# Attention transfers gathered on one queue, in the order of need

## The chip, the cores and the metric

The kernel runs on one core of a Trainium2 chip. The time is device microseconds of one execution. Five engines work side by side, each with its own instruction stream: TensorE (matrix products), VectorE, ScalarE, GpSimd and SyncE. In this kernel SyncE does nothing but start transfers between HBM and the on-chip memory (SBUF); ScalarE and GpSimd start some as well, between their computations. An engine starts its instructions in order, so an instruction that waits holds up all that stand behind it.

## The reference, cut to what matters

First a block-sparse attention over 4 sequences of 768 tokens with 8 heads of 64; a query block of 32 tokens sees its own block and both neighbours, the first and the last block of the sequence, and three sampled blocks:

```python
scores = scale * np.matmul(q, k.transpose(0, 1, 3, 2))
mask = np.abs(blk_i - blk_j) <= 1
mask = mask | (blk_i == 0) | (blk_j == 0) | (blk_i == n_blocks - 1) | (blk_j == n_blocks - 1)
for qb in range(n_blocks):
    for kb in sampled_blocks[qb]:
        mask[qb * 32:(qb + 1) * 32, kb * 32:(kb + 1) * 32] = True
scores = np.where(mask, scores, -1e9)
attn = softmax(scores)
x = np.matmul(attn, v)                      # then (B, H, S, D) -> (B*S, H*D): 3072 rows of 512
```

Then each of the 3072 rows goes to one of 8 experts, chosen by the cosine between the row and the experts' embeddings:

```python
expert_idx = np.argmax(xn @ en.T / tau, axis=1)
gate_w = softmax(...)[np.arange(N), expert_idx]
for e in range(E):
    mask = expert_idx == e
    h = np.maximum(x[mask] @ w1[e], 0.0)    # 512 x 1024
    out[mask] = gate_w[mask, None] * (h @ w2[e])
```

All is float32.

## The kernel before, in words

The attention walks over 24 chunks of 128 queries, six to a sequence. A chunk's rows are shifted by one block, so the first chunk of a sequence holds the last block and the first three. `attention_fast` has a loop over s from 0 to 24, and its order of instructions is written out by hand: no scheduler moves anything. One iteration s scores chunk s (`score_near`, `score_far`, with the exponentials on ScalarE at L534/L540 and L559), prepares the keys of the sampled blocks for chunk s+1 (`gather_k`, on GpSimd and VectorE, L495), weighs V for chunk s-1 (`weigh_near`, `weigh_far`, all TensorE instructions at L589), turns K of the next sequence one pair of heads at a time (`turn_k`, L464/L466), turns Q of chunk s+1 (`turn_q`, L478), and normalizes chunk s-1. In a sequence's first chunk the first and the last block attend to everything (`score_ends`, L576).

Data comes in these transfers. Q: 256 KB a chunk (`load_q`, L392), in two pieces for the first chunk of a sequence, issued by ScalarE two chunks ahead into two buffers (tile `qraw`). K: two transfers of 192 KB for a pair of heads (`load_k`, L401, tile `kraw`, two buffers), by SyncE for sequence 0 and by ScalarE afterwards. V twice: once whole for a sequence (`load_v`, ten transfers, tile `vst`; L1237 for sequence 0, L1319 by ScalarE afterwards, three at the end of each iteration), with the two end blocks in a second place too (`vg0`, which the profile lists as `vg`); and once more block by block for the sampled blocks (`gather_v`, L444, SyncE): 12 transfers of 64 KB for a chunk (6 for a sequence's first) into one of three `vg` buffers, at addresses that SyncE holds in registers. The registers are loaded from the tile `offset` (L379) when a chunk's place in the sequence comes up for the first time; the addresses of the first and third slot share one register (`PACK`) and are taken apart by a shift and a mask. `near_v` (L454) copies the neighbour blocks from `vst` into `vg` on GpSimd.

Once a sequence is through, its routing runs in small steps put into later iterations by a list (`after_sequence`); its last steps write the rows with their gate to HBM (`x_dram`, L789): seven transfers of up to 258 KB, by ScalarE during attention and by SyncE after it. After sequence 1 the first 5 tiles of 128 rows for the experts are laid out; the weights of the first come in iterations 20 to 22 in eight pieces (L1078, SyncE). Then follow the expert tiles: 64 products at L1125, 16 at L1140 for each, with 4 MB of weights a tile from SyncE, and rows in and out by indirect transfers from GpSimd (L1049, L1055, L1149). The experts' embedding and tau are loaded by SyncE (`load_experts`, L208/L210) after the gathers of chunk 0 and are normalized in `build_experts` in iterations 0 and 1.

Waits are set by the framework: a reader waits for the writer, and a transfer into a buffer for the buffer's last reader.

Of the kernel before, what the change touches and what calls it, by code (L numbers as in the profile page):

```python
# [26 lines left out]
PACK = 1024  # L27
# [305 lines left out]
def build_choice(k):  # L333
# [6 lines left out]
    k.offset = k.const.tile([P, NRAND + 1, NB], I32, name="offset")  # L340
    nc.vector.tensor_scalar(out=k.offset[:, 0:NRAND, 2:], in0=at, scalar1=float(BLK), scalar2=None, op0=ALU.mult)
    nc.vector.tensor_scalar(out=at, in0=at, scalar1=float(BLK), scalar2=None, op0=ALU.mult)
    nc.vector.scalar_tensor_tensor(out=k.offset[:, NRAND, 2:], in0=at[:, 2], scalar=float(PACK), in1=at[:, 0],
                                   op0=ALU.mult, op1=ALU.add)
# [28 lines left out]
def shifts(k, engine, s, c):  # L373

    blocks = blocks_of(c)
    key = engine, s, c
    if key not in k.shift:
        most = (S - BLK) * (PACK + 1 if s == NRAND else 1)
        _, values = k.nc.values_load_multi_w_load_instructions(  # L379
            k.offset[0:1, s, NG * c + blocks[0]:NG * c + blocks[-1] + 1], engines=(engine,), min_val=0, max_val=most,  # L380
            skip_runtime_bounds_check_because="the block numbers are clamped to the blocks there are")
        k.shift[key] = list(values)
    return k.shift[key]


def load_q(k, n):

    b, c = divmod(n, NC)
    k.raw["q", n] = t = k.ld.tile([P, H, D], F32, name="qraw", tag="qraw", bufs=2)
    src = k.q[b].rearrange("h s d -> s h d")  # L390
    for rows, lo in pieces(c):
        k.nc.scalar.dma_start(out=t[rows], in_=src[lo:lo + rows.stop - rows.start])  # L392


def load_k(k, g, pool=None):
# [3 lines left out]
    for h in range(2):  # L399
        engine = k.nc.scalar if b else k.nc.sync  # L400
        engine.dma_start(out=t[:, :, h], in_=k.k[b, 2 * j + h].rearrange("(c p) d -> p c d", p=P))  # L401


def load_v(k, b):

    v, vg0 = k.vst[b % 2], k.vg0[b % 2]
# [23 lines left out]
def gather_v(k, n):  # L430
# [1119 lines left out]
```

## Time and profile before

| | |
|---|---|
| median of three runs | 715.79 us (711.06 to 717.91) |
| the profiled execution, its time | 719.66 us |
| the profiled execution, its span | 717.9 us |
| TensorE busy | 636.9 us (89%) |
| VectorE, ScalarE, GpSimd busy | 222.5, 121.4, 233.3 us |
| first score of chunks 0, 6, 12, 18 | 20.0, 107.1, 185.2, 266.8 us |
| first expert product, last one's end | 343.3, 711.1 us |
| transfers on SyncE's queue (q1) | 135.52 MB, 57.1% of 16 DMA engines' span |
| on ScalarE's queue (q10) | 20.88 MB, 13.5% |

The span goes from the first instruction to the last. A line of the profile names an engine, a line of the kernel, what is written and read, and times; an engine's name with a q (SPq is SyncE's queue, ACTq ScalarE's) is its issuing part, whose time isn't counted as busy. PE is TensorE, PEld its weight loads, DVE VectorE, ACT ScalarE, POOL GpSimd. PEclk and the column after the engines' busy times are the clock granted to TensorE, 1.00 being full.

### The profile page before, as it was taken

How to read it: one execution, taken by the hardware profiler on the slowest of the kernel's cores; microseconds unless marked ns; L12 is line 12 of the kernel's file. 1: busy time of each engine (PE TensorE's matmuls, PEld its weight loads, DVE VectorE, ACT ScalarE, POOL GpSimd, SP SyncE). 2: the span in 40 equal slices, each digit the busy share in tenths (PEclk: the TensorE clock that was granted, in tenths of full speed). 3: DMA queues.
4: the chain of work that ended last, by engine and by line, in shares of the span. 5: the costliest groups of instructions: out<-in, count | busy, mean ns of one | idle time of the engine just before them, and what ended most of it. 6: DMA issues, size and time to landing. Idle time of an engine off the chain costs nothing.

```text
span 717.9 us, 21825 instructions
## 1 busy us (share of the span) xinstructions
PE 636.9 (89%) x9016; PEld 500.4 (70%) x9016; DVE 222.5 (31%) x663; ACT 121.4 (17%) x278; POOL 233.3 (33%) x444
## 2 busy tenths in 40 slices
PE   7487789787896879985899999999999999999996
PEld 4476788776885868874766777677467773677673
DVE  6442223352253436640256111211211121112110
ACT  2312214223322415321100000000000000000000
POOL 1552124241241424450020234224322432243232
PEclk8876669979798879996889999999999999999999
DMA  9846544688436854459799999999989999899911
GB/s 169 150 105 128 104 101 91 128 142 195 115 77 139 140 137 114 115 133 267 258 399 370 396 406 367 346 345 321 342 317 396 408 393 387 315 404 397 355 34 41
DMA packets 192191, 171.33 MB, mean 239 GB/s; under 512 B 152584, under 2 KB 152712, under 8 KB 189266
## 3 DMA queue, kind: packets, MB, share of 16 engines
q1 hardware_dynamic: 119938, 135.52, 57.1%
q10 hardware_dynamic: 66928, 20.88, 13.5%
q0 software_dynamic: 5216, 13.43, 5.2%
q8 instruction: 73, 1.20, 0.7%
q14 instruction: 36, 0.29, 0.1%
HBM read 157.17 MB, written 12.90 MB: 237 GB/s over the span
## 4 chain that ended last, share of the span: by engine, by line
PE 73%; DMA 13%; DVE 4%; issue 4%; ACT 2%; SPq 2%; ACTq 1%; POOL 1%; POOLq 0%; DVEq 0%
PE hp L1125 23%; PE yp L1140 22%; PE av L589 11%; DMA vg<-in_v_dram 4%; PE yp L696 4%; DMA kraw<-in_k_dram 4%; DMA qraw<-in_q_dram 3%; PE xg_ps L478 3%; PE hp L1168 2%; PE yp L1188 2%; DVE x L672 2%; DMA x_dram<-x 1%; PE bps L576 1%; PE kps L464 1%; PE dps L554 1%
## 5 line engine op out<-in xcount | busy, mean ns | idle before, releaser
L1125 PEld LDWEIGHTS hp<-xgt,w 128*128 128x128 f32 x1472 | 167.8, 192 | 10.2 <-issue 10.2
L1125 PE MATMUL hp<-xgt,w 128*128 128x128 f32 x1472 | 168.9, 276 | 0.0
L1140 PE MATMUL yp<-w,h 128*128 128x512 f32 x368 | 163.5, 598 | 0.0
L1140 PEld LDWEIGHTS yp<-w,h 128*128 128x128 f32 x368 | 69.0, 193 | 78.1 <-issue 77.8
L1049 POOL DMA_INDIRECT xg<-x_dram,quarter x88 | 88.5, 1006 | 32.3 <-issue 27.4
L495 POOL COPY kg<-kt 128x128 f32 x176 | 45.0, 300 | 85.5 <-issue 59.9
L1149 POOL DMA_INDIRECT out_dram<-y,slot_l x20 | 20.2, 1011 | 156.8 <-DVE y L1148 156.8
L454 POOL COPY vg<-vst 32x520 f32<-32x520 f32 x80 | 49.4, 618 | 59.0 <-PE av L589 29.5
L589 PE MATMUL av<-vg,pd 128*32 128x65 f32 x1408 | 39.4, 266 | 28.3 <-DMA vg<-in_v_dram 19.9
L1128 ACT ACTIVATE h<-hp 128x512 f32<-128x512 f32 x23 | 13.7, 597 | 291.5 <-PE hp L1125 291.5
L482 DVE COPY qt<-xg_ps 64x512 f32<-64x512 f32 x48 | 33.1, 689 | 96.0 <-PE xg_ps L478 95.2
L589 PEld LDWEIGHTS av<-vg,pd 128*32 128x32 f32 x1408 | 32.6, 137 | 35.0 <-issue 13.0
L1132 DVE TENSOR_SCALAR h<-hp 128x512 f32<-128x512 f32 x23 | 15.9, 691 | 127.9 <-PE hp L1125 127.9
L589 PE MATMUL av<-vst,pac 64*64 64x65 f32 x1056 | 51.7, 243 | 1.0 <-issue 0.7
L554 PE MATMUL dps<-qt,kg 128*64 128x64 f32 x1408 | 49.5, 231 | 0.6 <-issue 0.3
L554 PEld LDWEIGHTS dps<-qt,kg 128*64 128x64 f32 x1408 | 46.1, 145 | 2.6 <-issue 0.4
L1148 DVE TENSOR_SCALAR y<-yp,gate 128x512 f32<-128x512 f32 x20 | 15.0, 751 | 102.1 <-PE yp L1140 90.1
L589 PEld LDWEIGHTS av<-vst,pac 64*64 64x64 f32 x1056 | 43.9, 153 | 3.8 <-issue 1.4
L464 PE MATMUL kps<-ident,kraw 128*128 128x128 f32 x96 | 17.8, 335 | 22.2 <-ACT pac L534 21.1
L530 PE MATMUL ac<-qt,ke 64*64 64x128 f32 (+1 forms) x384 | 33.8, 311 | 1.6 <-ACT pd L559 0.9
L559 ACT ACTIVATE pd<-dps,bias 128x256 f32<-128x256 f32 x88 | 34.6, 476 | 1.5 <-PE dps L554 1.4
L696 PEld LDWEIGHTS yp<-en,xt 128*128 128x128 f32 x192 | 32.8, 257 | 2.1 <-ACT sq L677 1.2
(228 smaller groups left out, 659.3 us busy)
## 6 DMA issues: line engine op xcount, KB each, us to landing
w<-in_moe_w_dram SPq DMA_DIRECT2D x52, 2048.0 KB, 15.7
vg<-in_v_dram SPq DMA_DIRECT2D x266, 64.0 KB, 3.2
qraw<-in_q_dram ACTq DMA_DIRECT2D x20, 256.0 KB, 3.3
kraw<-in_k_dram ACTq DMA_DIRECT2D x24, 192.0 KB, 3.8
w<-in_moe_w_dram SPq DMA_DIRECT2D x8, 512.0 KB, 4.8
x_dram<-x ACTq DMA_DIRECT2D x15, 258.0 KB, 4.4
vst<-in_v_dram ACTq DMA_DIRECT2D x15, 256.0 KB, 4.7
kraw<-in_k_dram SPq DMA_DIRECT2D x8, 192.0 KB, 5.6
```

The source lines that it names most:

```text
L454: k.nc.gpsimd.tensor_copy(out=k.vg[n][NRAND * BLK:P, g], in_=k.vst[b % 2][rows, m])
L464: nc.tensor.transpose(ps[:, c // 3, c % 3 * P:(c % 3 + 1) * P], raw[:, c].rearrange("p h d -> p (h d)"), k.ident)
L482: k.nc.vector.tensor_copy(out=t[rows, :, h], in_=ps[rows])
L495: copy(out=t[:, :, g, s * BLK:(s + 1) * BLK], in_=kt[:, :, bass.ds(shift, BLK)])
L530: nc.tensor.matmul(ps[D * r:D * (r + 1), h, lo:lo + cols.stop - cols.start], lhsT=keys, rhs=qt[rows, j, h, cols], start=True, stop=True)
L554: nc.tensor.matmul(out[D * r:D * (r + 1), NG * j + g], lhsT=kg[:, j, g, D * r:D * (r + 1)], rhs=qt[:, j, :, cols], start=True, stop=True)
L559: nc.scalar.activation(e[:, :, g].rearrange("p j h t -> p j (h t)"), out.rearrange("p (j g) h t -> p j g (h t)", g=NG)[:, :, g], ACT.Exp, ...
L589: k.nc.tensor.matmul(av[lanes, h // NPAIR, h % NPAIR * P:h % NPAIR * P + D + 1], lhsT=lhsT, rhs=rhs, start=first[0], stop=last, skip_group ...
L696: k.nc.tensor.matmul(ps[:, 0:E], lhsT=xt[:, j], rhs=k.en[:, j, :], start=(j == 0), stop=(j == ND - 1))
L1049: k.nc.gpsimd.indirect_dma_start(out=x[:, g], out_offset=None, in_=quarters, in_offset=bass.IndirectOffsetOnAxis(ap=k.quarter[:, g, t:t + ...
L1125: nc.tensor.matmul(hp[:, f, :], lhsT=w1[:, d, (f0 + f) * P:(f0 + f + 1) * P], rhs=xt[:, d, :], start=(d == 0), stop=(d == ND - 1))
L1140: nc.tensor.matmul(yp, lhsT=h[:, f, :], rhs=w2[:, f, :], start=(f == 0), stop=(f == NF - 1))
```

## The change

Every transfer of the attention but the first two chunks' Q is issued by SyncE, at the head of an iteration and in the order in which the data is needed: K, Q, the sampled blocks of V, V of the next sequence; the row writes stay at their places in the list. Q is loaded three chunks ahead into three buffers instead of two. V of a sequence comes in seven transfers instead of ten: the last and the first block lie together in `vst`, and the second copy of the two end blocks is made on chip by GpSimd (`keep_ends`). For that the end blocks change places, and the end keys `ke` are copied by two ScalarE instructions instead of one. The rows of a sequence go to HBM in four transfers instead of seven (two of them over two and three chunks, 516 and 774 KB), in three steps of the list instead of six. The packed register is gone; the third slot's four addresses are loaded anew for each chunk. The experts' embedding is loaded before V of sequence 0.

```diff
-    k.offset = k.const.tile([P, NRAND + 1, NB], I32, name="offset")
+    k.offset = k.const.tile([P, NRAND, NB], I32, name="offset")
...
-    nc.vector.tensor_scalar(out=at, in0=at, scalar1=float(BLK), scalar2=None, op0=ALU.mult)
-    nc.vector.scalar_tensor_tensor(out=k.offset[:, NRAND, 2:], in0=at[:, 2], scalar=float(PACK), in1=at[:, 0],
-                                   op0=ALU.mult, op1=ALU.add)
...
+        if engine == mybir.EngineType.SP and s == NRAND - 1:
+            return list(values)
         k.shift[key] = list(values)
...
-    k.raw["q", n] = t = k.ld.tile([P, H, D], F32, name="qraw", tag="qraw", bufs=2)
+    k.raw["q", n] = t = k.ld.tile([P, H, D], F32, name="qraw", tag="qraw", bufs=3)
...
-        k.nc.scalar.dma_start(out=t[rows], in_=src[lo:lo + rows.stop - rows.start])
+        (k.nc.scalar if n < 2 else k.nc.sync).dma_start(out=t[rows], in_=src[lo:lo + rows.stop - rows.start])
...
-        engine = k.nc.scalar if b else k.nc.sync
-        engine.dma_start(out=t[:, :, h], in_=k.k[b, 2 * j + h].rearrange("(c p) d -> p c d", p=P))
+        k.nc.sync.dma_start(out=t[:, :, h], in_=k.k[b, 2 * j + h].rearrange("(c p) d -> p c d", p=P))
...
-    for i, at in enumerate((0, S - BLK)):
-        for lo, to in ((0, v[:, 0]), (D, vg0)):
-            parts.append((to[lo + i * BLK:lo + (i + 1) * BLK, :, 0:D], src[at:at + BLK]))
-    parts.append((v[D:P, 0, :, 0:D], src[BLK:BLK + D]))
+    parts.append((v[0:BLK, 0, :, 0:D], src[S - BLK:S]))
+    parts.append((v[BLK:P, 0, :, 0:D], src[0:P - BLK]))
...
+def keep_ends(k, b):
+
+    k.nc.gpsimd.tensor_copy(out=k.vg0[b % 2][D:P], in_=k.vst[b % 2][0:D, 0])
...
-        for g, shift in zip(blocks_of(c), shifts(k, mybir.EngineType.SP, s if s == 1 else NRAND, c)):
-            if s == 0:
-                shift = shift & (PACK - 1)
-            elif s == 2:
-                shift = shift >> (PACK.bit_length() - 1)
-            if s != 1:
-                shift.max_val = S - BLK
+        for g, shift in zip(blocks_of(c), shifts(k, mybir.EngineType.SP, s, c)):
...
-        nc.scalar.copy(out=k.ke[b % 2][:, pairs].rearrange("p j (n t) -> p j n t", n=2),
-                       in_=k.kt[b % 2][:, pairs].rearrange("p j (n t) -> p j n t", t=BLK)[:, :, 0:NB:NB - 1])
+        for i, block in enumerate((NB - 1, 0)):
+            nc.scalar.copy(out=k.ke[b % 2][:, pairs, i * BLK:(i + 1) * BLK],
+                           in_=k.kt[b % 2][:, pairs, block * BLK:(block + 1) * BLK])
...
-    queue = nc.scalar if k.attending else nc.sync
-    for c in range(NC):
-        for rows, lo in pieces(c, not k.exact):
-            queue.dma_start(out=k.x_dram[b * S + lo:b * S + lo + rows.stop - rows.start, :],
-                              in_=x[rows, c].rearrange("p e w -> p (e w)"))
+    for rows, lo in pieces(0, not k.exact):
+        nc.sync.dma_start(out=k.x_dram[b * S + lo:b * S + lo + rows.stop - rows.start, :],
+                          in_=x[rows, 0].rearrange("p e w -> p (e w)"))
+    yield
+    first = b * S + P - BLK * (not k.exact)
+    for some in (range(1, 3), range(3, NC)):
+        lo = first + P * (some.start - 1)
+        nc.sync.dma_start(out=k.x_dram[lo:lo + P * len(some), :].rearrange("(c p) w -> p c w", p=P),
+                          in_=x[:, some.start:some.stop].rearrange("p c e w -> p c (e w)"))
         yield
...
-    plan += [(s + 3 + (i // 2 + 1) // 2, (i // 2 + 1) % 2, routing) for i in range(NC)]
+    plan += [(s + 3 + (i + 1) // 2, (i + 1) % 2, routing) for i in range(3)]
...
         load_k(n, g, n.setup if g < 2 else None)
+    load_experts(n)
     for to, src in load_v(n, 0):
         nc.sync.dma_start(out=to, in_=src)
...
     near_v(n, 0)
-    load_experts(n)
+    keep_ends(n, 0)
...
+        if s == 0:
+            load_q(n, 2)
+            for g in range(NPAIR, NPAIR + 2):
+                load_k(n, g)
+        if b + 1 < B and c >= 2 and NPAIR * (b + 1) + c < B * NPAIR:
+            load_k(n, NPAIR * (b + 1) + c)
+        if s + 3 < NCH:
+            load_q(n, s + 3)
         if s + 1 < NCH:
             gather_v(n, s + 1)
+        if b + 1 < B and c:
+            for to, src in load_v(n, b + 1)[2 * c - 2:2 * c]:
+                nc.sync.dma_start(out=to, in_=src)
+        if b + 1 < B and c == 2:
+            keep_ends(n, b + 1)
         if s < NCH:
             score_near(n, s)
...
-        if s == 0:
-            for g in range(NPAIR, NPAIR + 2):
-                load_k(n, g)
-        if s + 2 < NCH:
-            load_q(n, s + 2)
-        if b + 1 < B:
-            g = NPAIR * (b + 1) + c + 1
-            if 1 <= c <= NPAIR and g < B * NPAIR:
-                load_k(n, g)
-            for to, src in load_v(n, b + 1)[3 * c:3 * c + 3]:
-                nc.scalar.dma_start(out=to, in_=src)
```

More of the change, by code (lines that the diff above doesn't have):

```diff
@@ L26 @@
 NC = S // P
-PACK = 1024
 NPAIR = H // 2
@@ L377, in shifts @@
     if key not in k.shift:
-        most = (S - BLK) * (PACK + 1 if s == NRAND else 1)
         _, values = k.nc.values_load_multi_w_load_instructions(
-            k.offset[0:1, s, NG * c + blocks[0]:NG * c + blocks[-1] + 1], engines=(engine,), min_val=0, max_val=most,
+            k.offset[0:1, s, NG * c + blocks[0]:NG * c + blocks[-1] + 1], engines=(engine,), min_val=0, max_val=S - BLK,
             skip_runtime_bounds_check_because="the block numbers are clamped to the blocks there are")
+        if engine == mybir.EngineType.SP and s == NRAND - 1:
+            return list(values)
         k.shift[key] = list(values)
@@ L399, in load_k @@
     for h in range(2):
-        engine = k.nc.scalar if b else k.nc.sync
-        engine.dma_start(out=t[:, :, h], in_=k.k[b, 2 * j + h].rearrange("(c p) d -> p c d", p=P))
+        k.nc.sync.dma_start(out=t[:, :, h], in_=k.k[b, 2 * j + h].rearrange("(c p) d -> p c d", p=P))
 def load_v(k, b):
-    v, vg0 = k.vst[b % 2], k.vg0[b % 2]
+    v = k.vst[b % 2]
     src = k.v[b].rearrange("h s d -> s h d")
     parts = []
-    for i, at in enumerate((0, S - BLK)):
-        for lo, to in ((0, v[:, 0]), (D, vg0)):
-            parts.append((to[lo + i * BLK:lo + (i + 1) * BLK, :, 0:D], src[at:at + BLK]))
-    parts.append((v[D:P, 0, :, 0:D], src[BLK:BLK + D]))
+    parts.append((v[0:BLK, 0, :, 0:D], src[S - BLK:S]))
+    parts.append((v[BLK:P, 0, :, 0:D], src[0:P - BLK]))
     for m in range(1, NC):
@@ L1244, in attention_fast @@
         nc.gpsimd.memset(n.vst[i][:, :, :, D:D + 1], 1.0)
-        nc.gpsimd.memset(n.vg0[i][D:P, :, D:D + 1], 1.0)
         nc.gpsimd.memset(n.qt_ring[i], 0.0)
```

## The prediction

> **What bounds the kernel now.** I read the forty slices first, then the stretches of the span cut at the attention's own borders, then who waited for whom, then the queues' timelines. The slices of the span:
>
> ```profile
> PE   7487789787896879985899999999999999999996
> ...
> PEclk8876669979798879996889999999999999999999
> ```
>
> TensorE is full in the right half (the experts) and runs there at the full clock; in the left half (attention, some 18 slices) it is at 7 to 8 tenths with the clock down to 6. The stretches give the same by sequence: prologue, sequences 0, 1, 2, 3, tail of the attention, experts.
>
> ```profile
> 20.00:107.10 87.10, 65.47 (x1401) 59.31 (x1401) 28.85 (x93) 21.97 (x53) 30.59 (x87) 0.74 0.59 117
> 107.10:185.20 78.10, 64.56 (x1742) 59.16 (x1740) 29.68 (x97) 25.49 (x61) 26.45 (x75) 0.87 0.67 136
> 185.20:266.80 81.60, 65.51 (x1743) 60.05 (x1742) 30.53 (x103) 25.92 (x61) 26.49 (x75) 0.86 0.58 125
> 266.80:336.20 69.40, 55.67 (x1689) 51.30 (x1690) 32.69 (x120) 23.50 (x57) 26.65 (x62) 0.89 0.57 145
> ...
> 359.40:711.20 351.80, 351.33 (x1969) 242.10 (x1967) 80.71 (x198) 15.75 (x27) 116.04 (x123) 1.00 0.91 343
> ```
>
> After the stretch come length, busy time of TensorE, its weight loads, VectorE, ScalarE, GpSimd, then granted clock, DMA share and GB/s. The experts (351.33 of 351.80 us busy at 1.00) can't gain from transfers. A sequence costs 70 to 87 us with 14 to 22 us of TensorE idle, and the busy part runs at 0.74 to 0.89. No other engine is near its length. The same view by chunk shows what a chunk costs undisturbed:
>
> ```profile
> 211.30:227.20 15.90, 11.03 (x265) 10.06 (x265) 6.11 (x22) 4.17 (x9) 1.94 (x8) 0.79 0.68 131
> ...
> 241.80:250.60 8.80, 8.80 (x256) 8.32 (x256) 4.52 (x18) 4.69 (x10) 1.98 (x6) 0.92 0.52 112
> ...
> 280.50:291.70 11.20, 11.20 (x314) 10.45 (x309) 7.43 (x27) 3.37 (x8) 5.71 (x11) 1.00 0.42 92
> 291.70:299.80 8.10, 7.57 (x255) 7.02 (x253) 5.98 (x24) 3.31 (x8) 2.52 (x3) 1.00 0.41 99
> ```
>
> The first and the second line are chunks of nearly the same work (both turn a pair of K): 15.90 us with 4.87 idle, and 8.80 with none. Why the first is late, ScalarE's timeline tells:
>
> ```profile
> 213.75 0.43 ACTq L392 DMA_DIRECT2D qraw<-in_q_dram  x1
> ...
> 214.22 2.12 ACTq L401 DMA_DIRECT2D kraw<-in_k_dram  x2
> 216.38 0.68 ACTq L1319 DMA_DIRECT2D vg<-in_v_dram  x1
> 217.71 2.22 ACTq L1319 DMA_DIRECT2D vst<-in_v_dram  x2
> 219.98 1.02 ACT L534 ACTIVATE pac<-ac 128x1024 f32<-128x1024 f32 x1 [5.61 <-DMA kraw<-in_k_dram]
> ```
>
> ScalarE issues Q, K and V for the next chunks and only then takes the exponential, L534, for which TensorE's next turn of K waits (they share two PSUM buffers). The second coupling is on SyncE, whose gathers of V (L444) wait here for:
>
> ```profile
> SPq L444 <- DMA qraw<-in_q_dram: 76.3, 17, 7.7
> SPq L444 <- DMA kraw<-in_k_dram: 33.4, 12, 9.2
> ...
> SPq L444 <- PE av L589: 2.2, 5, 0.9
> ```
>
> The gathers need neither Q nor K. But the trace shows eight landing semaphores (numbers 100, 102, 103, 105 to 109) passed round among SyncE's and ScalarE's transfers, and an issue waits until the last transfer on its semaphore has landed. So SyncE's gathers wait for transfers that ScalarE hasn't issued yet: 110 us in 29 waits, against 2.2 us for the buffers (PE av). TensorE in turn stands at L589 for V.
>
> **The change, part by part.**
>
> *Transfers off ScalarE.* A middle sequence has 28 to 30 of them, 17.5 us of its queue (17.48 and 17.64 us in sequences 1 and 2). ScalarE's compute in a sequence is 25.5 us, so it is no bound afterwards; the 5 us before each L534 go, and with them the waits of TensorE on pac (chunks 2 and 3 of each sequence: 2.7 to 4.9 us each).
>
> *All on SyncE.* A middle sequence then has 66 gathers, 7 Q, 8 K, 7 V (10 before), 4 token-row transfers (7 before): 92. The 264 gathers occupied the queue 112.05 us, 0.42 each (median 0.317; 29 of them took 0.8 to 2.0), and register moves around each 0.21: 66 x 0.64 = 42 us. The others at ScalarE's means: 7 x 0.45 + 8 x 0.69 + 7 x 0.72 + 4 x 0.45 = 15.5, with 0.05 between: 17. The third slot's addresses: 6 register loads of 0.30 (median of the TENSOR_LOADs on SyncE), 2 us; the shifts and masks that go give back 44 x 0.07 = 3, which I let stand against the loads' longest (0.69). Sum 61 us if nothing waits. Back to back large transfers on this one queue are slower:
>
> ```profile
> 1.27 9.56 SPq L401 DMA_DIRECT2D kraw<-in_k_dram  x8
> ...
> 13.39 7.12 SPq L1237 DMA_DIRECT2D vst<-in_v_dram  x6
> ```
>
> 18 transfers from 1.27 to 20.52 us, 1.07 each. At that price the 26 large ones are 27.8 and the sum 72. I take 64: the gathers between them leave DMA engines half idle (share 0.36 to 0.44 in chunks that mostly gather), so most of a backlog drains behind them.
>
> *TensorE's own floor.* The first chunk of a sequence: 12.0 us busy at 0.86 to 0.88, so 10.4 at 1.00, and 0.9 of short waits: 11.3. The second 11.2 (the third line above). The third and fourth 8.1 (the fourth line) and 1.0 for a turn of K (6 transposes at L464, 0.87 to 0.98 us undisturbed): 9.1 each. The fifth 8.8. The sixth 7.8 (313.4 to 321.2). Sum 57.3.
>
> *How they meet.* V of chunk n goes into one of three buffers. It can start when chunk n-3 is weighed and is wanted when chunk n is: three iterations, of which its own transfers take one. SyncE may thus run late by some 12 us before TensorE stands. 64 against 57.3 eats this in two sequences, so I set sequence 1 at 63 and sequence 2 at 64.
>
> *Sequence 0.* Today it contains 7.4 us at 28.6, when TensorE waits for the expert embedding (L230, ScalarE waits 9.6 us for its landing, issued at 31.75). Loaded before V, it is there by 16; of the 7.4 I keep 2 for the chain of ScalarE, GpSimd and VectorE behind it. The second K set now comes after the first gathers: 3 us lost. SyncE has 90 transfers there, 62 us from about 24. I set 67 for 87.1.
>
> *Sequence 3.* No K, no V: 66 gathers, 3 Q, 4 rows, 8 weight pieces at 0.4: 42 + 1.5 + 2 + 3.2 + 2 = 51 us of SyncE; TensorE 11.3 + 11.2 + 3 x 8 + 6.5 = 53. The 7.5 us at 326.6 come from gathers that wait for ScalarE's row transfers (landing after 5.9 us behind weights); I keep 3. Together 56 for 69.4.
>
> *Small parts.* Split copies of the end keys: 4 more of 0.25 us in the prologue, about 0.5 on the path; 3 more later, hidden by an idle ScalarE. Two small transfers ahead of V: 0.9 us, three V transfers fewer: nothing. The copy of the end blocks on GpSimd: four of 0.62 (L454's mean for the same 520 elements a partition). GpSimd is busy 26.5 us of 80 in a sequence, so this is hidden, but it waits for two V transfers, and behind it stand 8 copies of K for the next chunk (0.30 each) and TensorE's scores. V is issued a chunk ahead; if SyncE is 5 us late there, the copy is late too, some 3 us at each of three places. Row transfers of 516 and 774 KB: same bytes. Tail and experts: unchanged.
>
> Sum: 20.1 + 15.1 + 17.6 + 13.4 - 0.5 = 65.7 saved. The profiled run took 719.66 us, so 654; it lies 3.9 above the median of 715.79, which makes 650 for a median. I say 651.
>
> A rule that speaks about the price: in the Trainium skill, "DMA: Bandwidth & Descriptors", section "Issuing engines are not separate DMA queues", starting transfers from several engines saves only the time to initiate them, "usually small relative to the DMA itself". By it one queue costs nothing and a sequence stays at TensorE's floor, the sum then being the second rival's. The rows differ: a gather holds SyncE 0.64 us and lands after 3.2 (median), with eight in flight, so initiation is what would fill the queue. I go by the rows.
>
> **Rivals.**
>
> *SyncE is the bound throughout* (72 a sequence, and late copies on GpSimd). For it: 1.07 us in the prologue. Against: there all descriptors were large. Savings 11 + 6 + 10 + 8 = 35: 685 profiled, 681.
>
> *TensorE's floor throughout.* SyncE's slack is never used up. Savings 25 + 21 + 24 + 17 = 87: 633 profiled, 629. For it: undisturbed chunks exist; against: 61 us of issue with no wait at all.
>
> *Slower: one queue in order.* If every transfer, gathers too, waits behind the large ones at the prologue's 1.07 us, a sequence is 92 x 1.07 + 2 = 100 us (22 and 18 longer), sequence 0 is 90 x 1.07 + 4 = 100 (13 longer) and sequence 3 81 x 1.07 + 2 = 89 (19 longer): 72 us more, 788. It decides from (80 - 2) / 92 = 0.85 us a transfer on, where sequences 1 and 2 are as long as now. Against: 40 transfers from both queues, 17 of them large, went out between 160.8 and 184 us, 0.58 each, over the same eight semaphores.
>
> *No change.* The waits move from pac to L589 and nothing is won: 716. Against it stand the undisturbed chunks.
>
> **How the numbers follow.** Forecast (632 to 668) 0.58, SyncE-bound (668 to 705) 0.18, TensorE's floor (below 632) 0.11, no change 0.05, slower 0.08. The three first cases are faster: 0.87; 1% (7 us, what the three runs from 711.06 to 717.91 can tell) either way 0.04; slower 0.09. The range 628 to 694 leaves out the slower and unchanged cases and little else.
>
> **What would show it.** No transfer on ScalarE's queue in attention after the first Q; the 5 us before L534 gone; sequences of 62 to 65 us at a clock of 0.95 or more; SyncE's gathers waiting for V's own landings and not for Q. A mean step above 0.75 us between SyncE's transfers, or GpSimd's L454 and L495 waiting for V, means the SyncE-bound case. I am wrong if TensorE still idles over 10 us a sequence, or if the first weights come so late that the experts start with a gap.

## The result, and the profile after

The changed kernel takes 665.32 us (median of four runs, 662.58 to 666.76); the kernel before took 716.85 us on the same chip (711.06 to 724.82). The ratio is 0.930 [0.923, 0.937]; the slow run of 724.82 us before isn't counted in it. The profiled execution took 665.99 us against 719.66, 53.7 less; the forecast was 651 for the median, 654 for the profiled run.

The slices of the page, to be held against those before:

```profile
PE   7787988798969889798999999999999999999995
PEclk7897999799889989977999999999999999999999
```

In the left half, the attention, the clock now stands mostly at 9 tenths where it went from 6 to 9. It still isn't full: TensorE has 7s and 8s there, and so has the clock. The stretches (length; busy time of TensorE, its weight loads, VectorE, ScalarE, GpSimd; clock, DMA share, GB/s) for sequences 0 to 3, the tail of the attention, and the experts:

```profile
19.00:79.70 60.70, 50.74 (x1401) 46.30 (x1396) 31.23 (x96) 22.18 (x54) 32.09 (x90) 0.92 0.65 143
79.70:146.90 67.20, 57.55 (x1746) 53.63 (x1743) 29.94 (x97) 25.71 (x62) 26.72 (x76) 0.95 0.64 142
146.90:216.30 69.40, 58.78 (x1747) 54.45 (x1744) 31.06 (x104) 25.93 (x62) 27.14 (x77) 0.95 0.67 152
216.30:286.30 70.00, 59.33 (x1777) 54.17 (x1773) 35.98 (x125) 24.43 (x60) 27.38 (x64) 0.95 0.75 176
...
314.20:657.60 343.40, 342.22 (x1945) 237.67 (x1943) 76.32 (x184) 15.51 (x26) 113.26 (x113) 1.00 0.90 338
```

Counted to the first expert product, the sequences took 87.1, 78.1, 81.6 and 76.3 us before and take 60.7, 67.2, 69.4 and 69.8 now: 26.4, 10.9, 12.2 and 6.5 less. With 1.0 won in the prologue and 3.4 lost between the first expert product and the end (374.8 to 378.2 us) that is the whole difference. The saving has two parts: in sequences 0 to 2 TensorE's busy time fell from 195.5 to 167.1 us, for the same matmuls at a higher granted clock (0.74 to 0.87 before, 0.92 to 0.95 now), and its idle time from 51.3 to 30.2. No run varied the clock by itself.

The wait that the change was to remove is gone. SyncE's gathers of V (L444 before, L437 now) waited 76.3 us for Q and 33.4 for K; SyncE's waits now list, for Q, one of under a microsecond, and for K none:

```profile
SPq L437 <- DMA qraw<-in_q_dram: 0.8, 1, 0.8
```

What is left shows in the waits of the other engines over the attention (total, times, longest). L414 is the copy of V's end blocks on GpSimd (`keep_ends`), L489 the copies of sampled K behind it, L548 the scores that need them:

```profile
POOL vg L414 <- DMA vst<-in_v_dram: 63.1, 3, 23.1
...
PEld dps L548 <- POOL kg L489: 17.2, 6, 5.4
PE dps L548 <- POOL kg L489: 16.3, 6, 5.3
```

GpSimd stands three times for some 21 us, since two of V's transfers are late. The timeline of GpSimd in sequence 1:

```profile
118.42 0.61 POOL L414 COPY vg<-vst 64x520 f32<-64x520 f32 x1 [21.07 <-DMA vst<-in_v_dram]
119.09 1.95 POOL L489 COPY kg<-kt 128x128 f32 x8
```

TensorE stands 5.3, 5.0 and 4.4 us for this in chunks 3, 9 and 15, and the clock of those three chunks is 0.79 to 0.89. Chunk 9 alone takes 17.1 us where the forecast's sum had 9.1. Why V is late, SyncE's timeline tells:

```profile
105.13 8.31 SPq L437 DMA_DIRECT2D vg<-in_v_dram  x12
113.53 0.89 SPq L1285 DMA_DIRECT2D vst<-in_v_dram  x2
114.52 1.08 SPq L397 DMA_DIRECT2D kraw<-in_k_dram  x2
115.69 1.55 SPq L389 DMA_DIRECT2D qraw<-in_q_dram  x1
```

One transfer follows the other with about 0.1 us between the groups. Over the sequences 0, 1 and 2 SyncE waits 0.8, 0.7 and 0.7 us; the other 59.9, 66.5 and 68.7 us it is busy with 79, 90 and 91 transfers, 0.758, 0.739 and 0.755 us each. In the kernel before it waited 40.3, 32.5 and 38.3 us. (Counted are gaps of more than 0.15 us between its instructions; the profile's list of waits, which also takes in time inside an issue, gives 0.9, 3.3 and 1.5 us now.) SyncE is full.

### The profile page after: what moved, and what is told of

Same layout as the page of the kernel before. It is cut to its first block, busy times and chain, and to the rows that moved or that the text cites. A ratio compares the mean times of both kernels' runs of the same rounds, so it can differ in the third digit from the quotient of the medians.

```text
span 664.3 us, 21679 instructions
## 1 busy us (share of the span) xinstructions
PE 607.3 (91%) x9016; PEld 474.5 (71%) x9016; DVE 226.2 (34%) x661; ACT 122.3 (18%) x285; POOL 236.3 (36%) x446
## 4 chain that ended last, share of the span: by engine, by line
PE 73%; SPq 12%; issue 5%; DMA 3%; DVE 2%; ACT 1%; POOL 1%; POOLq 0%; ACTq 0%
PE hp L1123 25%; PE yp L1138 24%; SPq L437 9%; PE av L583 7%; PE dps L548 4%; DMA vst<-in_v_dram 3%; PE hp L1166 2%; PE yp L1186 2%; PE yp L690 2%; PE xg_ps L679 1%; PE ac L524 1%; PE xg_ps L472 1%; PE bps L570 1%; SPq L389 1%; SPq L374 1%
## 5 line engine op out<-in xcount | busy, mean ns | idle before, releaser
L1138 PEld LDWEIGHTS yp<-w,h 128*128 128x128 f32 x368 | 68.7, 192 | 77.6 <-issue 77.2
L1147 POOL DMA_INDIRECT out_dram<-y,slot_l x20 | 20.3, 1013 | 156.5 <-DVE y L1146 156.5
L548 PE MATMUL dps<-qt,kg 128*64 128x64 f32 x1408 | 52.7, 236 | 17.9 <-POOL kg L489 16.3
L548 PEld LDWEIGHTS dps<-qt,kg 128*64 128x64 f32 x1408 | 48.8, 149 | 20.5 <-POOL kg L489 17.2
L489 POOL COPY kg<-kt 128x128 f32 x176 | 45.3, 300 | 33.1 <-PE dps L548 11.4
L583 PE MATMUL av<-vst,pac 64*64 64x65 f32 x1056 | 48.6, 227 | 4.9 <-issue 4.6
L583 PEld LDWEIGHTS av<-vst,pac 64*64 64x64 f32 x1056 | 40.6, 139 | 4.9 <-issue 2.7
L1146 DVE TENSOR_SCALAR y<-yp,gate 128x512 f32<-128x512 f32 x20 | 15.0, 751 | 81.9 <-PE yp L1138 69.8
L681 DVE COPY xt<-xg_ps 128x512 f32<-128x512 f32 x24 | 16.6, 692 | 66.1 <-PE xg_ps L679 66.1
L583 PE MATMUL av<-vg,pd 128*32 128x65 f32 x1408 | 27.0, 224 | 5.6 <-issue 4.9
L583 PE MATMUL av<-vg,pac 64*64 64x65 f32 x352 | 30.0, 236 | 0.7 <-issue 0.6
L524 PE MATMUL ac<-qt,ke 64*64 64x128 f32 (+1 forms) x384 | 28.6, 275 | 1.7 <-ACT pd L553 0.9
L583 PEld LDWEIGHTS av<-vg,pd 128*32 128x32 f32 x1408 | 22.4, 110 | 10.1 <-issue 8.3
```

The costliest lines, as they stand in the source:

```text
L489: copy(out=t[:, :, g, s * BLK:(s + 1) * BLK], in_=kt[:, :, bass.ds(shift, BLK)])
L524: nc.tensor.matmul(ps[D * r:D * (r + 1), h, lo:lo + cols.stop - cols.start], lhsT=keys, rhs=qt[rows, j, h, cols], start=True, stop=True)
L548: nc.tensor.matmul(out[D * r:D * (r + 1), NG * j + g], lhsT=kg[:, j, g, D * r:D * (r + 1)], rhs=qt[:, j, :, cols], start=True, stop=True)
L583: k.nc.tensor.matmul(av[lanes, h // NPAIR, h % NPAIR * P:h % NPAIR * P + D + 1], lhsT=lhsT, rhs=rhs, start=first[0], stop=last, skip_group ...
L1138: nc.tensor.matmul(yp, lhsT=h[:, f, :], rhs=w2[:, f, :], start=(f == 0), stop=(f == NF - 1))
L1147: k.scattered = nc.gpsimd.indirect_dma_start(out=k.out[:, :], out_offset=bass.IndirectOffsetOnAxis(ap=slot, axis=0), in_=y[:, :], in_offse ...
```

## The experiments

Two readings of this profile lead to different repairs. Theory A: the copy of V's ends stands at a bad place, and moved it gives TensorE its 5 us back three times. Theory B: SyncE's queue sets the pace, the copy is only where TensorE notices, and any other place will show the wait elsewhere. The table sums up; the last columns are from the traces, in us: the lengths of sequences 0 to 2, and when the first expert product starts (343.1 in the kernel before; the 343.3 of the table above is 0.2 too late). The kernels ran in three groups and the last by itself, each beside the kernel before, whose median was 716.5 to 722.1 us in these; so times across groups are compared by their ratios and by the traces. There is one trace for each kernel, and it scatters: the edits of "embedding late" and "second K behind gathers" lie in sequence 0 alone, yet sequence 1 took 64.0 and 65.2 us in them against 67.2, and sequence 2 69.2 and 74.9 against 69.4. A few us in one sequence are no proof of what an edit does.

| kernel | median us | ratio to before | sequences 0, 1, 2 | first expert product |
|---|---|---|---|---|
| changed kernel | 665.3 | 0.930 [0.923, 0.937] | 60.7, 67.2, 69.4 | 286.1 |
| late copy | 666.0 | 0.928 [0.921, 0.935] | 62.8, 65.0, 68.3 | 283.5 |
| queue alone, old places | 688.2 | 0.958 [0.949, 0.968] | 76.4, 70.5, 70.8 | 307.9 |
| 66 tiny transfers more | 686.2 | 0.956 [0.946, 0.965] | 63.5, 71.2, 76.2 | 306.4 |
| late copy, V by GpSimd | 663.9 | 0.926 [0.918, 0.934] | 59.7, 65.3, 64.0 | 275.1 |
| late copy, V by ScalarE | 678.1 | 0.942 [0.932, 0.951] | 66.9, 70.5, 75.9 | 300.3 |
| embedding late | 665.6 | 0.927 [0.916, 0.938] | 62.3, 64.0, 69.2 | 284.0 |
| Q two ahead | 668.9 | 0.931 [0.922, 0.940] | 65.9, 64.5, 66.8 | 287.6 |
| gathers of half the size | 660.9 | 0.917 [0.908, 0.926] | 61.3, 63.4, 70.6 | 282.1 |
| two gathers of three | 672.5 | 0.934 [0.928, 0.941] | 51.9, 60.6, 61.4 | 261.8 |
| late copy, rows by GpSimd | 666.1 | 0.927 [0.921, 0.932] | 61.6, 69.3, 70.6 | 286.7 |
| new order, not fewer | 672.0 | 0.933 [0.926, 0.940] | 63.3, 66.8, 72.6 | 291.9 |
| second K behind gathers | 669.0 | 0.928 [0.922, 0.934] | 62.7, 65.2, 74.9 | 290.9 |

**The copy moved.** `keep_ends` goes from the head of a sequence's third iteration to the end of its fifth:

```diff
-        if b + 1 < B and c == 2:
-            keep_ends(n, b + 1)
...
+        if b + 1 < B and c == 4:
+            keep_ends(n, b + 1)
```

> The changed kernel with one step moved: GpSimd's copy of the end blocks comes at the end of the fifth chunk of a sequence instead of at the head of the third. Theory A (the copy): TensorE stands 5.3, 5.0 and 4.4 us before the scores of chunks 3, 9 and 15 because GpSimd's keys wait behind this copy and the copy for V; SyncE itself has slack. Then three waits of 5 us and some 2 us of slow clock behind each go: 20 us, 645. Theory B (SyncE): SyncE's queue is never idle (0.7 to 0.8 us of 61 to 69 in sequences 0 to 2), it issues no earlier when the copy moves, and TensorE runs ahead only to the next wait, for the gathered V: 0 to 5 us, 660 to 665, with new waits at the weighing line.

666.03 us: no gain. The waits at the copy are gone from the profile, and in TensorE's waits this line has come up in their stead:

```profile
PE kps L457 <- DMA kraw<-in_k_dram: 14.8, 6, 3.8
```

TensorE waits for K instead, up to 3.8 us, in chunks 1, 3, 4, 10, 15 and 16. Theory A falls.

**The queue alone.** The kernel before, its transfers at their old places and as many as they were, with ScalarE's issued by SyncE:

```diff
-        k.nc.scalar.dma_start(out=t[rows], ...)
+        (k.nc.scalar if n < 2 else k.nc.sync).dma_start(out=t[rows], ...)
-        engine = k.nc.scalar if b else k.nc.sync
+        engine = k.nc.sync
-    queue = nc.scalar if k.attending else nc.sync
+    queue = nc.sync
-                nc.scalar.dma_start(out=to, in_=src)
+                nc.sync.dma_start(out=to, in_=src)
```

> The kernel before with nothing changed but the engine: K, Q, V and the rows go out from SyncE, at their old places at the end of an iteration, Q two chunks ahead, V in ten and rows in seven transfers. Theory B: 98 transfers a middle sequence at 0.74 us are 73 us, for 78 and 82 before; with sequence 0 near 80 and sequence 3 near 72 the time is 690 to 700: a third to a half of the gain. Theory A: ScalarE's freedom is the gain and SyncE has slack, so all but the 5 us of the earlier embedding: about 670. A third, that the order at the head of the iteration makes the gain: 710 or more.

688.22 us: 28 of the 51 us come from the queue alone. TensorE's waits in this kernel (L478 turns Q, L464 turns K):

```profile
PE xg_ps L478 <- DMA qraw<-in_q_dram: 23.8, 8, 4.7
...
PE kps L464 <- DMA kraw<-in_k_dram: 8.1, 1, 8.1
```

Q and the second set of K come late here, 32 us in all. Theory B came nearest (690 to 700), but the run can't say yet whether the other 23 us lie in the order or in the count of transfers. Nor does it divide the 28: it frees ScalarE as well as the shared semaphores. In the kernel before TensorE had stood about as long for ScalarE's late exponentials as for V, and both are nearly gone here:

```profile
PE kps L464 <- ACT pac L534: 21.1, 7, 4.9
PE av L589 <- DMA vg<-in_v_dram: 19.9, 9, 7.5
```

**More transfers.** The changed kernel with 66 transfers of 64 bytes more:

```diff
+        if 0 < s < NCH - 1:
+            for i in range(3):
+                nc.sync.dma_start(out=n.tiny[i], in_=n.emb[0:1, 0:16])
```

> The changed kernel with three more transfers of 64 bytes on SyncE in each of chunks 1 to 22, behind the gathers: issue time without bytes, 66 in all. Theory B: each costs what an issue costs, 0.4 to 0.5 us, on a full queue: 26 to 33 us longer, 690 to 698. Theory A: SyncE's slack takes them: 665 to 670.

686.16 us; the first expert product is 20.3 us later, 0.31 us for each transfer that moves nothing. In the trace such an issue occupies SyncE 0.28 us, with a few hundredths after it: all of it comes through to the first expert product. The waits at the copy go from 5.3, 5.0 and 4.4 us to 4.9, 7.8 and 8.6. The time is a little under theory B's bounds, for which a tiny transfer had been put too dear; theory A's 665 to 670 is out of reach.

**V by GpSimd.** The late copy, with V of the next sequence (21 transfers in all) taken from SyncE:

```diff
-                nc.sync.dma_start(out=to, in_=src)      # ahead of score_near
...
+        if b + 1 < B and c:
+            for to, src in load_v(n, b + 1)[2 * c - 2:2 * c]:
+                nc.gpsimd.dma_start(out=to, in_=src)    # behind turn_q
```

> The late copy, and V of the next sequence issued by GpSimd behind its copies for the next chunk instead of by SyncE: 21 transfers in all leave SyncE's queue (7 a sequence, at 0.75 us: 5 us each in sequences 0 to 2). Theory B: 15 us less on the full queue beside the late copy's own gain: 640 to 650, clearly below the late copy alone. Theory A: SyncE had slack, so no different from the late copy alone, or slower by GpSimd's own issues (1 us each for its indirect transfers).

663.93 us, by the ratios (0.926 and 0.928) the same as the late copy alone: a miss for theory B by the time, and a hit for theory A, but the trace shows that SyncE had no slack. Attention does gain, 8.4 us of the 15 of theory B, with the clock at 0.97 in sequences 1 and 2:

```profile
78.70:144.00 65.30, 57.61 (x1747) 53.35 (x1744) 30.83 (x98) 25.81 (x62) 33.14 (x84) 0.97 0.75 150
144.00:208.00 64.00, 57.09 (x1743) 52.68 (x1740) 31.45 (x104) 25.82 (x62) 32.75 (x84) 0.97 0.83 166
```

The experts start at 275.1 us against 283.5 with the late copy. But from TensorE's last product to the end of the span there are now 13.5 us, and 6.8 without. A DRAIN instruction of GpSimd near the end takes 6.4 us in this trace and 1.1 in the changed kernel's; the last instructions of all other engines come after it. Of 8.4 us won, 6.7 go there.

**V by ScalarE.** The same transfers on ScalarE, behind its copy of K, where it has time:

```diff
             turn_k(n, g)
+        if b + 1 < B and c:
+            for to, src in load_v(n, b + 1)[2 * c - 2:2 * c]:
+                nc.scalar.dma_start(out=to, in_=src)
```

> The changed kernel with the copy of V's ends at the end of chunk 4, as in the run with the late copy, and with V of the next sequence (7 transfers a sequence, 21 in all) issued by ScalarE after it has copied K, where it then waits 1.6 to 3.3 us for the router's product. Theory B (SyncE's queue is full, 0.74 us a transfer): 7 fewer a sequence are up to 5 us; TensorE then sets the pace at about 64 us a sequence, the experts start at 275 to 279 us as with GpSimd issuing V, and without GpSimd's longer drain at the end (6.4 us there, 1.1 otherwise) the time is 651 to 657. Rival C (TensorE's own stalls already set the pace, so SyncE's relief brings nothing): 663 to 667, as with the late copy alone. Rival D (ScalarE's issues, some 0.5 to 1.2 us each, hold the next exponents as before the change): over 667, with waits for ScalarE ahead of the routing or the scoring.

678.07 us: by the ratios 10 us slower than the late copy alone, with intervals that just overlap, and by the traces 17 at the first expert product, though SyncE has 21 transfers fewer. Rival D's number, but not its reason: ScalarE isn't late. SyncE's own waits show it:

```profile
SPq L437 <- DMA vst<-in_v_dram: 38.9, 12, 6.6
...
SPq L397 <- DMA vst<-in_v_dram: 4.4, 1, 4.4
```

This is the second coupling of the prediction, back again with another tile. A gather takes one of the eight landing semaphores that the two queues pass round in program order. The gather that would have gone out at 99.8 us uses semaphore 109, whose turn before is that of a V transfer on ScalarE. ScalarE issues that at 103.8, and the gather goes out at 106.41, after 6.6 us. SyncE stands 14.3, 19.1 and 14.7 us in three sequences, and TensorE then waits 7.4 to 7.6 us for K in chunks 3, 9 and 15. So a part of the change's gain lies in the one order, whichever engine issues: with all transfers on one queue, the transfer that last had the semaphore has always been issued. GpSimd's transfers use other semaphores, which is why the run before this one has no such wait.

**The embedding late, and Q two ahead.** Two parts of the change, each undone by itself:

```diff
-    load_experts(n)          # ahead of V of sequence 0
...
+    load_experts(n)          # behind near_v and keep_ends of chunk 0
```

> The changed kernel with the experts' embedding loaded where it was before, behind the first gathers. The prediction's step 5 put the embedding at 5.4 us (a wait of 7.4 us in chunk 1 falling to 2). Theory A (this wait comes back, and nothing after it absorbs it): 669 to 673, chunk 1 some 4 to 6 us longer. Theory B (SyncE is full, and whatever TensorE waits in the first sequence is time in which SyncE gets ahead): 664 to 668, the wait comes back by 4 to 6 us but later waits in the first sequence, 5.3 us at the copy of V's ends, shrink by as much.

```diff
-    ... name="qraw", tag="qraw", bufs=3)
+    ... name="qraw", tag="qraw", bufs=2)
...
         if s == 0:
-            load_q(n, 2)
...
-        if s + 3 < NCH:
-            load_q(n, s + 3)
+        if s + 2 < NCH:
+            load_q(n, s + 2)
```

> The changed kernel with Q two chunks ahead in two buffers, the rest as changed. SyncE issues as many transfers. Theory B (the count of transfers on the full queue decides): 664 to 669. Rival, the order theory (Q a chunk earlier is what the new order buys; with the queue at the old places TensorE waited 2 to 4.7 us for Q in seven chunks, 23 us in all): 675 to 688, with TensorE waiting for Q ahead of turning it.

665.58 us for the first: nothing. Chunk 1 has 1.6 us of wait for the embedding, against 1.8 in the changed kernel, so not even the wait comes back; nor does the wait at the copy in chunk 3 shrink, as theory B had it (7.3 us). 668.85 us for the second, by the ratio the same as the changed kernel and within theory B's range. TensorE waits for Q now, and no longer for the copy in chunks 9 and 15:

```profile
PE xg_ps L472 <- DMA qraw<-in_q_dram: 15.7, 4, 5.5
```

It is the third place at which the same lateness of SyncE shows: the copy in the changed kernel, K with the late copy, Q here.

**Bytes or transfers.** Two kernels that gather less, the first in smaller transfers, the second in fewer:

```diff
-            ...dma_start(out=t[lanes, g, :, 0:D], in_=src[bass.ds(shift, BLK)])
+            ...dma_start(out=t[lanes, g, 0:H // 2, 0:D], in_=src[bass.ds(shift, BLK), 0:H // 2])
```

> The changed kernel with every gather of V cut to the first 4 of its 8 heads: as many transfers, half the bytes and half the 256-byte descriptors of each gather. It leaves out half of the random blocks' values. Theory B1 (a transfer costs SyncE a fixed sum, 0.3 us for a 64-byte one, plus its register and semaphore instructions): 661 to 666. Theory B2 (the long issues, a mean of 0.50 us for a gather against a median of 0.32, come from the descriptors still outstanding): most of 0.18 us by 66 gathers a sequence goes, 8 to 10 us in a sequence of which TensorE's own 64 lets 3 to 5 through: 645 to 655.

```diff
-    for s in range(NRAND):
+    for s in range(NRAND - 1):
```

> The changed kernel without the gathers of the third sampled block: 22 of 66 gathers a sequence go, with their register loads. It leaves out a third of the sampled blocks' values, and no work of TensorE. Theory B (SyncE's queue is full and sets the pace): SyncE falls to some 50 us a sequence, the 4.4 to 5.3 us at the copy of V's ends go, sequences 1 and 2 fall from 67 and 69 to 61 to 64 us, which is TensorE's own work with its own stalls: 645 to 655. Rival (the pace is TensorE's already, and the full queue only follows it): sequences of 66 to 70 us, 660 to 667.

With half the bytes and half the pieces in 66 gathers a sequence the experts start 4.0 us earlier and the time is 660.94, beside the 661 to 666 of theory B1; the intervals of the two ratios overlap. With a third of the gathers gone they start 24.2 us earlier. Its stretches, sequences 0 to 2:

```profile
19.20:71.10 51.90, 47.88 (x1398) 43.68 (x1394) 31.69 (x96) 22.15 (x54) 30.77 (x88) 1.00 0.69 152
71.10:131.70 60.60, 55.99 (x1744) 52.35 (x1742) 30.28 (x98) 25.69 (x62) 27.37 (x77) 0.97 0.71 157
131.70:193.10 61.40, 56.92 (x1748) 52.79 (x1745) 31.26 (x104) 25.79 (x62) 27.29 (x77) 0.97 0.64 152
```

TensorE does the same work (1744 and 1748 matmuls), in sequences of 60.6 and 61.4 us, as theory B had it; the waits at the copy are under a microsecond, and SyncE waits again, 3.8 and 11.2 us. The 672.46 us of the whole can't be compared: with other values the rows spread otherwise over the experts, 1616 products into `hp` where there were 1552, one tile more and a gap of 10.7 us ahead of it. So it is the number of transfers that fills SyncE, and hardly their bytes.

**Rows by GpSimd.** The drain was long with V, which moves in pieces of 256 bytes; the rows move in pieces of 2 KB:

```diff
+    queue = nc.gpsimd if k.attending else nc.sync
-        nc.sync.dma_start(out=k.x_dram[...], in_=...)
+        queue.dma_start(out=k.x_dram[...], in_=...)
```

> The changed kernel with the late copy and with the rows written by GpSimd during attention (4 transfers a sequence, about 1.0 us of SyncE each; three sequences). GpSimd's transfers use other semaphores than SyncE's. Theory B: 4 us less of SyncE in each of three sequences, of which TensorE lets 2 to 3 through in two; the rows are long (2 KB), so few descriptors, and GpSimd's drain at the end grows by less than 1 us (with 21 transfers of V it grew by 5.3): 657 to 662. Rival (the drain goes by the number of GpSimd's transfers, or GpSimd's own work is late): 664 to 670.

666.14 us: no gain. The drain is indeed shorter (8.8 us from the last product to the end, 2.0 more than without), but the attention isn't: the experts start at 286.7 us, 3.2 later than with the late copy alone. SyncE's 85 transfers of sequence 1 take it 68.7 us, 0.81 each (0.73 with the late copy alone). Theory B in its simple form, 0.74 us for every transfer taken away, fails here, and why those 85 took longer stays open.

**What the order is worth.** The new order, Q three ahead and the embedding early, but V in ten transfers, rows in seven and the packed register as before: the kernel of the queue alone, with its loads at the head of an iteration as in the changed kernel.

> The kernel before with all its transfers on SyncE's queue in the changed order, Q three chunks ahead and the embedding early, but with V in ten transfers, rows in seven and the packed register as before: the changed kernel with 24 more transfers, and the shifts and masks. Theory B (the count on the full queue decides): 24 by 0.74 us and 3 us a sequence of shifts and masks, of which some are hidden: 678 to 688, near the 688 of the queue alone at the old places. Rival (order theory: the 22 us between that run and the changed kernel come from the order and from Q further ahead): 664 to 671.

672.0 us. By the times, 16 of the 23 us that were open come from the order, 7 from 24 fewer transfers and the register; by the ratios, 2.5% and 0.3%, the second within the intervals. Theory B had said 678 at least: its price of 0.74 for one more transfer is too high here too; the order theory's 664 to 671 is missed by 1. Of the 16 us the traces put 13 in sequence 0 (76.4 to 63.3 us). The last run undoes one step of it:

```diff
         if s == 0:
             load_q(n, 2)
-            for g in range(NPAIR, NPAIR + 2):
-                load_k(n, g)
...
         if s + 1 < NCH:
             gather_v(n, s + 1)
+        if s == 0:
+            for g in range(NPAIR, NPAIR + 2):
+                load_k(n, g)
```

> The changed kernel with one step of its order undone: the second set of K (4 transfers, wanted in chunk 1) stands behind the 12 gathers of iteration 0, not ahead of them. With all transfers on SyncE at the old places TensorE waited 8.1 us for this K in chunk 1, and the first sequence was 13 us longer than in the run with the new order and the same number of transfers. Theory O (this one place is most of what the order brings): TensorE waits 5 to 8 us for K in chunk 1, the first sequence is 5 to 12 us longer, 670 to 677. Rival (whatever is lost there is given back by the next wait of the first sequence, as with the late embedding, or it was the sum of many places): 664 to 668.

668.98 us, between the two, and by the ratio (0.928) as the changed kernel. The wait is there as foreseen:

```profile
PE kps L457 <- DMA kraw<-in_k_dram: 8.8, 1, 8.8
```

But the first sequence is only 2.0 us longer: while TensorE stands 8.8 us in chunk 1, SyncE goes on, and the 5.3 us at the copy in chunk 3 don't occur (the third sequence is longer instead, with 7.1 us at the copy in chunk 15, which nothing in this edit explains). A single late item is paid back at the next wait. That the order is nevertheless worth 16 us with Q, K and the rest all late together is measured; how that sum divides wasn't tried further.

No variant is faster than the changed kernel by more than these runs can tell.

## Why the prediction was right, and where its sum was off

**What bounds: right.** The waits of gathers for Q and K through the shared semaphores were named; putting 21 transfers back on ScalarE brought waits of the same kind, 43 us of them on SyncE, and a later start of the experts. ScalarE's late exponentials were named too. Taking both away brought 28 us; how these divide wasn't tried. "Gathers waiting for V's own landings", as the text expected, hardly occurs: they wait for nothing, because SyncE never gets ahead.

**SyncE's price: mis-sized, and the cause of the miss.** The sum had 66 gathers at 0.64 and 19 us for the rest, 61, taken as 64. Measured: 66.5 and 68.7 us. In these two sequences a gather's issue took 0.504 us (the sum had 0.42), K and Q 0.78 instead of 0.69 and 0.45, a row transfer 1.06 instead of 0.45, and V 0.49 instead of 0.72. The median gather is unchanged, 0.317: the means are raised by long issues, of which the last section tells. The 64 was 2.5 and 4.7 short, the 72 of the SyncE-bound rival 5.5 and 3.3 over. The rival's first sign, a mean step above 0.75 us, came at its border (0.74 to 0.76); its second, GpSimd waiting for V, came in full. One reading that spoke for a quick queue was wrong: between 160.8 and 184 us the kernel before sends 34 transfers, 12 of them large, 0.69 us each, not 40 at 0.58. The outcome is the rival's mechanism at a price between the two, 14 us above the forecast and 16 below the rival.

**TensorE's floor and the slack: the floor too low.** 57.3 us a sequence; with SyncE relieved of 22 gathers TensorE still takes 60.6 and 61.4. Nearly all of the difference lies in a sequence's first chunk: set at 11.3, it took 14.4 and 15.4 us there, and 13.8 and 14.5 in the changed kernel, with 3 to 4 us idle where the sum had 0.9 of short waits. (The sixth chunk's 7.8 was read from a fifth chunk, 313.4 to 321.2; it came out as 7.8 and 8.2 with fewer gathers, 8.6 and 8.7 in the changed kernel.) The distance from queue to floor was about as foreseen (64 less 57.3 is 6.7; measured, 66.5 and 68.7 less 61, 5.5 and 7.7), both being some 4 us higher. But the slack of 12 us was not eaten in sequences 1 and 2, as the sum had it, for SyncE was late from the start: the last gather of chunk 1 goes out 14.5 us after that chunk's first score, those of chunks 6 and 12 15.2 us after. It had also been counted for the gathers of V, and SyncE's lateness showed from chunk 3 on at the transfers with the least lead. So sequences 1 and 2, set at 63 and 64, took 67.2 and 69.4, and TensorE was idle 9.7 and 10.6 us in them, about the 10 that the text had named as the sign of an error. The clock came to 0.92 to 0.95, not above.

**The small part that wasn't.** "If SyncE is 5 us late there, the copy is late too, some 3 us at each of three places": it was 5.3, 5.0 and 4.4. It had been left out of the sum. The run with the late copy (no gain) shows that it is the place of the wait, not its cause, and no sum of its own.

**Sequence 0: better than set,** 60.7 for 67, and not by the step named. Undone one at a time, the early embedding, K ahead of the gathers and the third Q made this sequence 1.6, 2.0 and 5.2 us longer in their one trace each; the embedding had been counted at 5.4, K as a loss of 3. TensorE's 7.4 us of wait for the embedding went with the queue: with the queue alone, the embedding at its old place, it was 1.9. Without any of the new order it is 13 us longer than with all of it. A part is only put off: of the 90 transfers counted for this sequence 79 go out in it. These 6.3 us more than set are luck as far as the sum goes: they hide a third of the 19.9 us by which sequences 1 to 3 and the end fell short. Without them the median would be near 672, outside the forecast's 632 to 668.

**Sequence 3: the worst term.** 13.4 us were expected from it, 6.5 came. SyncE does wait there (6.8 us), so it isn't full. Chunk 18 took 13.2 us for 11.3, chunk 19 took 15.5 for 11.2, with a gap of 2.8 us and the clock at 0.89: 6.2 of the 6.9 us that are missing. The forecast took no account of such gaps of TensorE (below).

**The end: 3.4 us lost** where nothing was to change, in the first 35 us after the first expert product (120 products take 34.3 us, 31.3 before). With the rows on GpSimd they took 31.3, but 33.7 and 32.9 in two other variants with the rows on SyncE, so that it is the rows' transfers beside the first tile's is a guess.

**Initiation as a cost.** By the Trainium skill, "DMA: Bandwidth & Descriptors", section "Issuing engines are not separate DMA queues", initiation is "usually small relative to the DMA itself". By the trace a gather's issue, 0.317 us at the median, is indeed small beside the 3.2 us to its landing in the kernel before, and the queue fills all the same. The rows were the better guide: 66 transfers that moved 64 bytes each made the kernel 20 us longer.

## What to carry to other kernels

Transfers on two engines' queues that share landing semaphores wait for each other in program order; look for an issue that waits for a tile it doesn't use, and bring such transfers onto one queue before you look for a faster engine. Then count what that one queue does: transfers by their mean issue time, not by the median, and not by their bytes. Redo the mean on the queue as it will be: here 0.42 us a gather became 0.50. When a queue is full, the wait moves with every repair (here copy, K, Q); don't add up the waits, take work off the queue, and check what the other queue costs at the end.

## What the runs showed of the hardware that was not expected

**SyncE's long issues end with instruction fetches.** The trace lists 53 transfers of 16 KB on the instruction queue (q8) between 19 and 286 us, 1.04 us each (median). Of the 263 gathers in that time, 59 are under way when such a fetch ends or runs; their issue takes 0.93 us on average. The other 204 take 0.35. The long ones end 0.39 us after the fetch (quartiles 0.39 and 0.40). The kernel before shows the same 0.39, with 28 long ones; 21 more of its 53 fetches end while SyncE waits. Over all of SyncE's transfers of the changed kernel this is 51 us beyond the usual 0.3 to 0.4, some 13 a sequence. It goes some way to explain why the mean step is 0.74 us while one transfer more or less moved the first expert product by 0.24 to 0.40 in four runs (tiny ones 20.3 us by 66, two gathers of three 24.2 by 88, V by GpSimd 8.4 by 21 against the late copy, 24 more in the new order 5.8; the rows by GpSimd are the exception): much of the difference would be a fixed sum. The fetches stay at 53 with 66 transfers more on SyncE or 88 fewer. In that time TensorE has 13425 of the core's 15754 instructions and SyncE 990, so most must be TensorE's if each brings as many; whose they are wasn't tested, nor that the fetch is what holds the issue.

**TensorE has gaps after such fetches.** Eleven gaps of 0.7 to 2.8 us, 15.1 us together, for which the profile names no wait, all end 1.2 to 1.7 us after a fetch ends. The longest, in chunk 19:

```profile
234.28 0.59 PE L583 MATMUL av<-vg,pd 128*32 128x65 f32 x25
237.67 0.32 PE L583 MATMUL av<-vg,pd 128*32 128x65 f32 x7 [2.80 <-issue]
```

The Trainium skill, "Runtime: NRT & Kernel Launch", section "Instruction fetch mechanics", says that instructions are refilled in blocks of 16 KB, which agrees with the size here, and that crossing a block costs a tail bump, "mostly hidden". In this kernel the gaps behind fetches come to some 4 us a sequence on TensorE and the long issues to 13 on SyncE, which isn't hidden: here the measurement decides.

**GpSimd's queue is paid for at the end.** 21 transfers of V in 256-byte pieces lengthened the time between the last product and the end by 6.7 us, 12 of rows in 2 KB pieces by 2.0. Whether this goes by pieces, transfers or bytes can't be told from two runs.

**Many pieces on one queue.** Take the transfers of sequences 0 to 2 that no fetch overlaps, and call an issue long if it takes over 0.45 us for a gather, over 0.6 for another transfer. Of 18 that began with 1900 or more 256-byte pieces still outstanding on SyncE's queue (bytes issued less bytes moved), 15 were long; of the other 182, 6. With gathers of half the size it is 17 of 24 and 1 of 177, so the smaller gathers didn't remove them; most are large transfers behind large ones.
